# Lightning attention and a Fourier mix on one core: two plain groups of the perceptron and five Strassen pairs, with each batch's mix beside the next batch's attention

## The chip, the cores and the metric

The kernel runs on one core of a Trainium2 chip. The metric is the device time in microseconds of one execution; the median of repeated runs is used. Engines are called by their short names: PE is TensorE's matmuls, PEld its loads of the stationary operand, DVE VectorE, ACT ScalarE, POOL GpSimd, SP the engine that issues most transfers.

## The reference, cut to what matters

```python
# q, k, v: (4 batches, 8 heads, 768 rows, 64) float32; lam: one decay per head
def _attn_ref(q, k, v, lam):                       # cut: set-up of Dmask, lam_pow, rev_pow
    for b in range(nb):                            # blocks of rows, a state carried along
        intra = np.einsum('bhic,bhjc->bhij', qb, kb) * Dmask[None]
        intra = np.einsum('bhij,bhjd->bhid', intra, vb)
        inter = np.einsum('bhid,bhde->bhie', qb * lam_pow[None], kv_state)
        out[:, :, sl] = intra + inter
        kv_state = lam_block * kv_state + np.einsum('bhsd,bhse->bhde', kb * rev_pow[None], vb)

def _moe_ref(x, w_ch1, w_ch2):                     # x: attention's result as (4, 768, 512)
    X = np.fft.fft(np.fft.fft(x, axis=1), axis=2)
    u = x + np.real(X)
    un = (u - mean(u)) / sqrt(var(u) + 1e-06)      # over the 512 columns of a row
    ch = np.maximum(un @ w_ch1, 0.0) @ w_ch2       # w_ch1 (512, 2048), w_ch2 (2048, 512), 64-bit
    return u + ch
```

So there are three parts for each of the four batches: attention, a Fourier mix with a normalisation, and a perceptron with one hidden layer of 2048.

## The kernel before

All matmuls are in 32-bit floats, each of them two records in the trace. Attention goes in chunks of 128 rows, six to a batch. The mix uses the symmetry of the real Fourier transform: rows and columns are folded (sums and differences of a row and its mirrored row), then come small matmuls with cosine and sine tables over the rows (L483), then over the columns (`width`). Mirrored rows come by an indirect gather from a copy in DRAM; for batch 0 they are made by turned transposes instead.

The perceptron works on groups of 256 rows: three to a batch, (batch, group) in the order `ORDER`. *Plain* groups are computed as the reference has it: 64 matmuls of 256 columns for the hidden layer and 32 of 512 columns for the second, woven into the rest of the kernel. *Late* groups are written to DRAM, normalised and transposed, and are computed at the end in pairs by Strassen's form (Winograd's variant): seven products of half size in place of eight, for both layers, with sums of the weights (`combine_weights`) and of the inputs made first on VectorE.

The kernel is a set of Python generators which yield an estimate of the time of each step; `weave` runs two of them side by side in the proportion given. What the generators give is the order of the program; a scheduler then places the instructions on the engines, and may move an instruction past others unless it is marked to stay in order.

```python
    xp = plain_pool("xp", 2 * NC)          # NC = 6: twelve buffers of 128 rows of x
    up = plain_pool("up", 3)
    # ... cut ...
    def attn(b):

        head = attn_in(b, 0)
        for c in range(NC):
            yield from head
            head = attn_in(b, c + 1) if c < NC - 1 else ()
            yield from attn_out(b, c, head)
    # ... attn_in: loads of k, q, v; transposes (L268, L273); attn_out: scores (L292, L296), state
    #     (L307 to L312), output (L320, L324), transposes back (L340); cut ...

    def fold_x(b, a, n, i, lo, hi):

        e, o = eo[b][a]
        tt = nc.vector.tensor_tensor

        tc.keep_in_program_order(tt(e[0:n, i, 0:DM], lo, hi, op=ALU.add))
        tc.keep_in_program_order(tt(o[0:n, i, 0:DM], lo, hi, op=ALU.subtract))
        tt(e[0:n, i, 1:HM], e[0:n, i, 1:HM], e[0:n, i, HM:DM - 1], op=ALU.add)
        tt(o[0:n, i, 1:HM], o[0:n, i, 1:HM], o[0:n, i, HM:DM - 1], op=ALU.subtract)

    # ... fold_a folds with rows mirrored inside the batch's second half, fold_b the other half and
    #     then the columns: eight more VectorE instructions for each of two blocks of rows; cut ...

    def fft_ln(b):
        yield 1.0
        fold_a(b)
        yield 3.0
        piece = fold_b(b)
        yield 6.0 if b == 0 else 9.0
        # ... matmuls with the tables, the widths, sums into x, norm for each group; cut ...

    ORDER = [(b, g) for b in range(B) for g in (1, 2, 0)]
    PLAIN, LATE = ORDER[:4], ORDER[4:]
    # ... cut ...
    def mlp(b, g, f0=0, f1=FO):

        ut = uts[b, g]
        hr = []
        for fc in range(f0, f1):
            ps = psum_m([128, G * 128])
            for c in range(KO):
                nc.tensor.matmul(ps, lhsT=w1[:, c, 128 * fc:128 * fc + 128], rhs=ut[:, c, :],
                                 start=(c == 0), stop=(c == KO - 1))
            if fc % 4 == 0:
                hr.append(new(hp_, [128, 4, G * 128], "hr"))
            t = hr[-1][:, fc % 4, :]
            if fc % 2:
                nc.vector.tensor_scalar(t, ps, 0.0, None, op0=ALU.max)
            else:
                nc.scalar.activation(t, ps, AF.Relu)
        # ... second matmul (L614) and the sum with x; with half of the hidden layer the sum goes
        #     back into x (L621, L622), at the end into y and out (L625, L626); cut ...

    # the conversion of the 64-bit weights: 32 pieces, each two ACT and five DVE instructions
    w = weights()
    t_chunk = 7.3
    t_front = NC * t_chunk + 13.0 + 7.0 + 5.7 + 3 * 2.4
    t_mlp = FO * 1.7 + G * 4 * 3.4
    def beside(lead, t, other, t_other):
        return weave(lead, part(other, t_other), t_other / t)

    att1, mix = attn(1), fft_ln(0)
    run(beside(attn(0), NC * t_chunk, w, 0.25 * NW))

    next(mix)
    run(beside(part(att1, t_chunk), t_chunk, w, 0.03 * NW))
    next(mix)
    run(beside(part(att1, t_chunk), t_chunk, w, 0.03 * NW))
    next(mix)
    run(part(att1, 0.5 * t_chunk))
    run(beside(mix, 24.0, beside(att1, 3.5 * t_chunk, w, 0.19 * NW), 0.19 * NW + 2.5 * t_chunk))

    half = [[mlp(b, g, h * FO // 2, (h + 1) * FO // 2) for b, g in PLAIN[:3]] for h in range(2)]
    fr = chain([att1, fft_ln(1)] + [front(b) for b in range(2, B)])
    t_rest, t_back = 3 * t_front - 5 * t_chunk, len(PLAIN) * t_mlp - 45.0
    t_half = 1.5 * t_mlp
    run(beside(beside(chain(half[0]), t_half, w, 0.5 * NW), t_half + 0.5 * NW, fr, t_rest * t_half / t_back))
    run(w)
    back = chain(half[1] + [mlp(*PLAIN[3])])
    run(weave(fr, back, (t_back - t_half) / (t_rest - t_rest * t_half / t_back)))
    front_end.close()
    s2.wp = ctx.enter_context(tc.tile_pool(name="ws", bufs=1, side="left", reuse_waits="tile"))
    # ... pools for the late groups are opened; load_u(0) ...
    run(weave(combine_weights(0), back, 1.5))
    run(back)
    # ...
    run(combine_weights(1))
    for j in range(len(LATE) // 2):
        late(j)
```

The buffers of x of a plain group are held until its second half has been added and stored; those of a late group are stored in DRAM right after its normalisation and become free.

Of the kernel before, what the change touches and what calls it, by code (L numbers as in the profile page):

```python
# [76 lines left out]
def kernel(  # L77
# [10 lines left out]
    nc = tc.nc  # L88
    B, H, S, D = q.shape
    DM = H * D  # L90
    DFF = moe_w_ch1.shape[1]
    C = 128
    NC = S // C
# [24 lines left out]
    def plain_pool(name, bufs):  # L118
        return plain_end.enter_context(tc.tile_pool(name=name, bufs=bufs, side="right"))
# [6 lines left out]
    np_ = front_pool("np", 2)  # L126
    ep = front_pool("ep", 2)
    xp = plain_pool("xp", 2 * NC)
    up = plain_pool("up", 3)
    hp_ = plain_pool("hp", FO // 4)  # L130
    dram = ctx.enter_context(tc.tile_pool(name="dram", bufs=1, space=bass.MemoryType.DRAM))
    PS = bass.MemoryType.PSUM
# [107 lines left out]

    def attn(b):

        head = attn_in(b, 0)
        for c in range(NC):
            yield from head
            head = attn_in(b, c + 1) if c < NC - 1 else ()
            yield from attn_out(b, c, head)

    ins, oTs, eo = {}, {}, {}
    TURNED = (0,)  # L250
    first = const.tile([128, HP, 1], F32, name="first")

    def attn_in(b, c):
        rows = slice(c * C, (c + 1) * C)
        kt, qt, vt = (new(ld, [C, H, D], nm) for nm in ("k", "q", "v"))
        for t, src in ((kt, k), (qt, q), (vt, v)):
            nc.sync.dma_start(t, src[b, :, rows, :].rearrange("h p d -> p h d"))
        if b == 0:
            load_tables(c)

        kd = None
        if c < NC - 1:
            kd = new(at, [C, H, D], "kd")
            nc.gpsimd.tensor_tensor(kd, kt, kpow, op=ALU.mult)

        ptk = psum_a([128, HP, C])
        for hp in range(HP):
            nc.tensor.transpose(ptk[:, hp, :], pair(kt, hp), ident)  # L268
        kT = new(at, [128, HP, C], "kT", bufs=2)
        nc.scalar.copy(kT, ptk)  # L270
        ptq = psum_a([128, HP, C])
        for hp in range(HP):
            nc.tensor.transpose(ptq[:, hp, :], pair(qt, hp), ident)  # L273
        qT = new(at, [128, HP, C], "qT", bufs=2)
        nc.scalar.copy(qT, ptq)  # L275
        qs = None
        if c > 0:
            qs = new(at, [128, HP, C], "qs")
            nc.vector.tensor_tensor(qs, ptq, qpow, op=ALU.mult)
        ins[b, c] = kT, qT, qs, kd, vt  # L280
        yield 1.2
# [123 lines left out]
# [4 lines that stand above are left out]

        tc.keep_in_program_order(tt(e[0:n, i, 0:DM], lo, hi, op=ALU.add))  # L410
        tc.keep_in_program_order(tt(o[0:n, i, 0:DM], lo, hi, op=ALU.subtract))
        tt(e[0:n, i, 1:HM], e[0:n, i, 1:HM], e[0:n, i, HM:DM - 1], op=ALU.add)
        tt(o[0:n, i, 1:HM], o[0:n, i, 1:HM], o[0:n, i, HM:DM - 1], op=ALU.subtract)

    def mirror_a(b):

# [15 lines left out]

    def fold_a(b):
        for a, n in enumerate(BLK):
            fold_x(b, a, n, 1, eo[b][a][1][0:n, 1, 0:DM], xn_[b, HC + a][0:n])

    def fold_b(b):

        sets = []
        tt = nc.vector.tensor_tensor  # L440
        for a, n in enumerate(BLK):
            fold_x(b, a, n, 0, xs[b, a][0:n], xs[b, HC + a][0:n])
            e, o = eo[b][a]
            nc.scalar.copy(e[0:n, :, HM:HM + 1], e[0:n, :, DM - 1:DM])

            am, bm = e[0:n, :, W:2 * W], o[0:n, :, W:2 * W]
            lo, hi = e[0:n, 0, 0:HM + 1], e[0:n, 1, 0:HM + 1]
            tt(am[:, 0, 0:HM + 1], lo, hi, op=ALU.add)
            tt(am[:, 1, 0:HM + 1], lo, hi, op=ALU.subtract)

            lo, hi = am[:, :, 0:QM], am[:, :, HM:QM:-1]
            tt(e[0:n, :, 0:QM], lo, hi, op=ALU.add)
            tt(e[0:n, :, QM:HM], lo, hi, op=ALU.subtract)
            lo, hi = o[0:n, 0, 1:HM], o[0:n, 1, 1:HM]
            tt(bm[:, 0, 1:HM], lo, hi, op=ALU.subtract)
            tt(bm[:, 1, 1:HM], lo, hi, op=ALU.add)
            lo, hi = bm[:, :, 1:QM + 1], bm[:, :, HM - 1:QM - 1:-1]
            tt(o[0:n, :, 0:QM], lo, hi, op=ALU.subtract)
            tt(o[0:n, :, QM:HM], lo, hi, op=ALU.add)
            sets.append((e, o))  # L460
        eo.pop(b)

        def piece(a, i, n):

            c0 = W + QM if i == 4 else QM * (i % 2)
            return sets[a][i in (2, 3)][0:BLK[a], n, c0:c0 + (1 if i == 4 else QM)]

        return piece

    def fft_ln(b):  # L470
        yield 1.0
        fold_a(b)
        yield 3.0
        piece = fold_b(b)
        yield 6.0 if b == 0 else 9.0


        for i in range(5):
# [101 lines left out]


    ORDER = [(b, g) for b in range(B) for g in (1, 2, 0)]
    PLAIN, LATE = ORDER[:4], ORDER[4:]

    def store(b, T, y, cols=slice(0, DM)):
        if T < HC:
            nc.sync.dma_start(out[b, 128 * T:128 * T + 128, cols], y[:, cols])
        else:
            nc.gpsimd.indirect_dma_start(out=out.rearrange("b s d -> (b s) d"),  # L589
                                         out_offset=row_of(2 + HC * (b + 1) + T - HC),  # L590
                                         in_=y[:, :], in_offset=None)

    def mlp(b, g, f0=0, f1=FO):

        ut = uts[b, g]
        hr = []
        for fc in range(f0, f1):
            ps = psum_m([128, G * 128])
            for c in range(KO):
                nc.tensor.matmul(ps, lhsT=w1[:, c, 128 * fc:128 * fc + 128], rhs=ut[:, c, :],  # L600
                                 start=(c == 0), stop=(c == KO - 1))
            if fc % 4 == 0:
                hr.append(new(hp_, [128, 4, G * 128], "hr"))
            t = hr[-1][:, fc % 4, :]
# [4 lines that stand above are left out]
            yield 1.7  # L609
        for i in range(G):  # L610
            T = TT[g][i]
            ps = psum_m([128, DM])
            for fc in range(f0, f1):
                nc.tensor.matmul(ps, lhsT=hr[(fc - f0) // 4][:, fc % 4, 128 * i:128 * i + 128], rhs=w2[:, fc, :],  # L614
                                 start=(fc == f0), stop=(fc == f1 - 1))
                if fc % 4 == 3 and fc < f1 - 1:
                    yield 3.4
            u = xs[b, T]
            tt = nc.vector.tensor_tensor
            if f1 < FO:  # L620
                tt(u[:, 0:HM], ps[:, 0:HM], u[:, 0:HM], op=ALU.add)  # L621
                tt(u[:, HM:DM], ps[:, DM - 1:HM - 1:-1], u[:, HM:DM], op=ALU.add)  # L622
            else:
                y = new(up, [128, DM], "y", bufs=1)
                tt(y[:, 0:HM], ps[:, 0:HM], u[:, 0:HM], op=ALU.add)  # L625
                tt(y[:, HM:DM], ps[:, HM:DM], u[:, DM - 1:HM - 1:-1], op=ALU.add)  # L626
                store(b, T, y)
            yield 3.4
# [138 lines left out]
    def front(b):  # L767
        yield from attn(b)
        yield from fft_ln(b)

    def weave(lead, other, ratio):

        t_lead = t_other = 0.0
        for d in lead:
            t_lead += d
            while t_other < t_lead * ratio:
                d = next(other, None)
                if d is None:
                    return t_lead + sum(lead)
                t_other += d  # L780
                yield d
            yield d
        return t_lead

    def run(gen):
        return sum(gen)

    def part(gen, n):
        for d in gen:
            yield d  # L790
            n -= d
            if n <= 0:
                return

    def chain(gens):
        for g in gens:
            yield from g
# [7 lines left out]
    def beside(lead, t, other, t_other):  # L805
        return weave(lead, part(other, t_other), t_other / t)
# [1 line left out]
    att1, mix = attn(1), fft_ln(0)  # L808
    run(beside(attn(0), NC * t_chunk, w, 0.25 * NW))

    next(mix)
    run(beside(part(att1, t_chunk), t_chunk, w, 0.03 * NW))
    next(mix)
    run(beside(part(att1, t_chunk), t_chunk, w, 0.03 * NW))
    next(mix)
    run(part(att1, 0.5 * t_chunk))
    run(beside(mix, 24.0, beside(att1, 3.5 * t_chunk, w, 0.19 * NW), 0.19 * NW + 2.5 * t_chunk))

    half = [[mlp(b, g, h * FO // 2, (h + 1) * FO // 2) for b, g in PLAIN[:3]] for h in range(2)]
    fr = chain([att1, fft_ln(1)] + [front(b) for b in range(2, B)])  # L820
    t_rest, t_back = 3 * t_front - 5 * t_chunk, len(PLAIN) * t_mlp - 45.0
    t_half = 1.5 * t_mlp
    run(beside(beside(chain(half[0]), t_half, w, 0.5 * NW), t_half + 0.5 * NW, fr, t_rest * t_half / t_back))
    run(w)
    back = chain(half[1] + [mlp(*PLAIN[3])])
    run(weave(fr, back, (t_back - t_half) / (t_rest - t_rest * t_half / t_back)))
    front_end.close()
    s2.wp = ctx.enter_context(tc.tile_pool(name="ws", bufs=1, side="left", reuse_waits="tile"))
    s2.up = ctx.enter_context(tc.tile_pool(name="us", bufs=1, side="left", reuse_waits="tile"))
# [43 lines left out]
```

## Time and profile before

| | |
|---|---|
| time, median of 3 runs | 843.8 us (843.48 to 846.13) |
| span of the profiled execution | 842.3 us |
| mean granted clock of TensorE | 0.988 |
| PE, PEld busy | 96%, 76% |
| DVE, ACT, POOL busy | 53%, 22%, 9% |
| data moved | 68.87 MB, mean 82 GB/s |
| hidden layer of plain groups (L600), PE busy | 119.8 us, 512 records |
| second layer of plain groups (L614), PE busy | 116.1 us, 256 records |
| Strassen products (L687 and L734) in the chain that ended last | 23% and 23% |

A group of instructions in the profile has a line of the kernel, an engine, its output and inputs by name, and a count. A group's busy time is the time in which at least one of its instructions ran, so matmuls that overlap in the array are not counted twice. The chain that ended last is followed back from the last instruction: at each step to the one that released it, or to the one before it on its engine.

### The profile page before, as it was taken

How to read it: one execution, taken by the hardware profiler on the slowest of the kernel's cores; microseconds unless marked ns; L12 is line 12 of the kernel's file. 1: busy time of each engine (PE TensorE's matmuls, PEld its weight loads, DVE VectorE, ACT ScalarE, POOL GpSimd, SP SyncE). 2: the span in 40 equal slices, each digit the busy share in tenths (PEclk: the TensorE clock that was granted, in tenths of full speed). 3: DMA queues.
4: the chain of work that ended last, by engine and by line, in shares of the span. 5: the costliest groups of instructions: out<-in, count | busy, mean ns of one | idle time of the engine just before them, and what ended most of it. 6: DMA issues, size and time to landing. Idle time of an engine off the chain costs nothing.

```text
span 842.3 us, 11685 instructions
## 1 busy us (share of the span) xinstructions
PE 805.3 (96%) x4608; PEld 642.3 (76%) x4608; DVE 446.0 (53%) x1030; ACT 181.9 (22%) x436; POOL 77.2 (9%) x102
## 2 busy tenths in 40 slices
PE   5987799999999999999999999999999999999998
PEld 4766676776767666767846888888888888888886
DVE  5969989884923483246696661155412552145411
ACT  3753442422521111221101210022000220012100
POOL 2211122010101110121000000000000000000000
PEclk9988999999999999999999999999999999999999
DMA  9957544137932125451334011100111000110010
GB/s 228 262 141 185 154 123 148 51 85 193 223 97 62 50 67 128 98 140 53 77 86 150 0 51 38 46 18 0 51 51 51 0 1 13 47 41 1 1 38 25
DMA packets 126683, 68.87 MB, mean 82 GB/s; under 512 B 111150, under 2 KB 112174, under 8 KB 126630
## 3 DMA queue, kind: packets, MB, share of 16 engines
q1 hardware_dynamic: 121632, 55.67, 26.1%
q0 software_dynamic: 2112, 6.69, 2.5%
q10 hardware_dynamic: 2886, 5.77, 2.0%
q8 instruction: 36, 0.59, 0.3%
q14 instruction: 17, 0.14, 0.1%
HBM read 48.72 MB, written 19.40 MB: 81 GB/s over the span
## 4 chain that ended last, share of the span: by engine, by line
PE 80%; DVE 10%; issue 4%; DMA 3%; ACT 2%; POOL 1%; SPq 0%; POOLq 0%; DVEq 0%; ACTq 0%
PE p L734 23%; PE p L687 23%; PE pm L614 9%; PE pm L600 7%; PE pa L292 3%; PE pa L324 3%; PE pa L483 3%; PE pa L320 2%; PE pa L340 1%; DMA x<-xb,ix 1%; PE pa L268 1%; PE pa L307 1%; PE pa L273 1%; DVE stt L513 1%; DMA xb<-xn 1%
## 5 line engine op out<-in xcount | busy, mean ns | idle before, releaser
L600 PE MATMUL pm<-ut,w 128*128 128x256 f32 x512 | 119.8, 383 | 0.2 <-DVE hr L606 0.2
L614 PE MATMUL pm<-w,hr 128*128 128x512 f32 x256 | 116.1, 598 | 1.3 <-DVE hr L606 1.3
L600 PEld LDWEIGHTS pm<-ut,w 128*128 128x128 f32 x512 | 94.1, 190 | 15.6 <-issue 3.4
L687 PE MATMUL p<-ur,w 128*128 128x256 f32 x384 | 93.8, 379 | 0.0
L614 PEld LDWEIGHTS pm<-w,hr 128*128 128x128 f32 x256 | 46.6, 190 | 51.4 <-issue 48.6
L687 PEld LDWEIGHTS p<-ur,w 128*128 128x128 f32 x384 | 73.0, 190 | 10.3 <-issue 0.5
L687 PE MATMUL p<-us,w1s 128*128 128x256 f32 x256 | 65.7, 379 | 0.0
L734 PE MATMUL p<-w,hs 128*128 128x256 f32 x256 | 58.0, 379 | 0.5 <-DVE y L755 0.5
L734 PE MATMUL p<-w,ha 128*128 128x256 f32 x256 | 57.9, 379 | 0.0
L734 PE MATMUL p<-w2s,hs 128*128 128x256 f32 x256 | 57.9, 379 | 0.0
L734 PEld LDWEIGHTS p<-w,hs 128*128 128x128 f32 x256 | 48.5, 190 | 7.5 <-DVE y L755 0.9
L734 PEld LDWEIGHTS p<-w,ha 128*128 128x128 f32 x256 | 48.6, 190 | 6.6
L734 PEld LDWEIGHTS p<-w2s,hs 128*128 128x128 f32 x256 | 48.6, 190 | 6.6
L687 PEld LDWEIGHTS p<-us,w1s 128*128 128x128 f32 x256 | 48.6, 190 | 6.6
L589 POOL DMA_INDIRECT out_dram<-y,ix x12 | 11.8, 987 | 408.4 <-DVE y L760 344.2
L714 ACT COPY ha<-p 128x256 f32<-128x256 f32 x32 | 11.9, 372 | 169.2 <-PE p L687 139.4
L292 PEld LDWEIGHTS pa<-qT,kT 64*128 64x128 f32 x384 | 29.2, 205 | 18.3 <-ACT qT L275 10.9
L292 PE MATMUL pa<-qT,kT 64*128 64x128 f32 x384 | 34.3, 306 | 8.0 <-ACT qT L275 7.5
L296 DVE TENSOR_TENSOR sc<-pa,decay 128x512 f32<-128x512 f32 x48 | 31.6, 682 | 12.7 <-PE pa L292 12.6
L725 DVE TENSOR_TENSOR ha<-p,ha 128x256 f32<-128x256 f32 x32 | 13.6, 425 | 44.8 <-ACT ha L724 44.8
L324 PE MATMUL pa<-sc,v 128*64 128x128 f32 x384 | 31.9, 288 | 4.5 <-DVE sc L296 4.5
L324 PEld LDWEIGHTS pa<-sc,v 128*64 128x64 f32 x384 | 23.4, 141 | 13.6 <-DVE sc L296 7.6
(144 smaller groups left out, 1143.2 us busy)
## 6 DMA issues: line engine op xcount, KB each, us to landing
raw<-in_moe_w_ch_dram SPq DMA_DIRECT2D x32, 512.0 KB, 5.0
k<-in_k_dram SPq DMA_DIRECT2D x24, 256.0 KB, 5.3
q<-in_q_dram SPq DMA_DIRECT2D x24, 256.0 KB, 5.0
v<-in_v_dram SPq DMA_DIRECT2D x24, 256.0 KB, 3.3
ud<-x SPq DMA_DIRECT2D x16, 256.0 KB, 2.3
utd<-e SPq DMA_DIRECT2D x64, 64.0 KB, 2.2
u<-ud SPq DMA_DIRECT2D x16, 256.0 KB, 2.7
ur<-utd SPq DMA_DIRECT2D x6, 512.0 KB, 4.7
```

What stands on the lines that cost most here:

```text
L292: mm(pss[hi][:, hp, :], lhsT=kT[HD[hi], hp, :], rhs=qT[HD[hi], hp, :], start=True, stop=True)
L296: nc.vector.tensor_tensor(t, pss[hi], decay[:, hi::2, :], op=ALU.mult)
L320: mm(po[HD[hi], hp, :], lhsT=s_old[HD[hi], hp, :], rhs=qs[HD[hi], hp, :], start=(hp == 0), stop=False, skip_group_check=True)
L324: mm(po[HD[hi], hp, :], lhsT=vt[:, 2 * hp + hi, :], rhs=sc[hi][:, hp, :], start=(c == 0 and hp == 0), stop=(hp == HP - 1), skip_group_chec ...
L483: mm = nc.tensor.matmul(ps[0:m, n, :], lhsT=piece(a, i, n), rhs=cs[0:rows, a, i in (2, 3), n, :], start=(a == 0), stop=(a == 1))
L589: nc.gpsimd.indirect_dma_start(out=out.rearrange("b s d -> (b s) d"), out_offset=row_of(2 + HC * (b + 1) + T - HC), in_=y[:, :], in_offset ...
L600: nc.tensor.matmul(ps, lhsT=w1[:, c, 128 * fc:128 * fc + 128], rhs=ut[:, c, :], start=(c == 0), stop=(c == KO - 1))
L614: nc.tensor.matmul(ps, lhsT=hr[(fc - f0) // 4][:, fc % 4, 128 * i:128 * i + 128], rhs=w2[:, fc, :], start=(fc == f0), stop=(fc == f1 - 1))
L687: nc.tensor.matmul(ps, lhsT=s2.A[a][:, kt, 128 * i:128 * i + 128], rhs=U[b][:, kt, :], start=(first and kt == 0), stop=(kt == 1), skip_gro ...
L714: nc.scalar.copy(a11, two(X))
L725: V.tensor_tensor(a22, two(Z), a22, op=ADD)
L734: nc.tensor.matmul(ps, lhsT=h[a][:, s, i, :], rhs=s2.B[b][:, i, :], start=(first and i == 0), stop=(i == HF - 1), skip_group_check=True)
```

## The change

Two of the twelve groups stay plain, (0, 1) and (0, 2), and the other ten are computed in five pairs in Strassen's form, which needs fewer products. The plain groups were what TensorE did while a mix went through its chain of folds, small matmuls and norms; in their place the mixes of batches 1 and 2 are now woven with the first three and a half chunks of the next batch's attention. For batch 0 the folds are handed out in small steps, with two and a half chunks of batch 1's attention beside them and no conversion of weights, and the first loads and transposes of batch 1 are made within the last chunk of batch 0. The hidden-layer matmuls of the second halves of the plain groups are marked to stay in program order.

```diff
--- before.py
+++ after.py
@@ -126,7 +126,7 @@
     np_ = front_pool("np", 2)
     ep = front_pool("ep", 2)
     xp = plain_pool("xp", 2 * NC)
-    up = plain_pool("up", 3)
+    up = plain_pool("up", 2)
     hp_ = plain_pool("hp", FO // 4)
     dram = ctx.enter_context(tc.tile_pool(name="dram", bufs=1, space=bass.MemoryType.DRAM))
     PS = bass.MemoryType.PSUM
@@ -240,13 +240,14 @@
 
     def attn(b):
 
-        head = attn_in(b, 0)
+        head = () if b - 1 in LEADS else attn_in(b, 0)
         for c in range(NC):
             yield from head
-            head = attn_in(b, c + 1) if c < NC - 1 else ()
+            head = attn_in(b, c + 1) if c < NC - 1 else attn_in(b + 1, 0) if b in LEADS else ()
             yield from attn_out(b, c, head)
 
     ins, oTs, eo = {}, {}, {}
+    LEADS = (0,)
     TURNED = (0,)
     first = const.tile([128, HP, 1], F32, name="first")
 
@@ -409,8 +410,10 @@
 
         tc.keep_in_program_order(tt(e[0:n, i, 0:DM], lo, hi, op=ALU.add))
         tc.keep_in_program_order(tt(o[0:n, i, 0:DM], lo, hi, op=ALU.subtract))
+        yield 1.4
         tt(e[0:n, i, 1:HM], e[0:n, i, 1:HM], e[0:n, i, HM:DM - 1], op=ALU.add)
         tt(o[0:n, i, 1:HM], o[0:n, i, 1:HM], o[0:n, i, HM:DM - 1], op=ALU.subtract)
+        yield 0.8
 
     def mirror_a(b):
 
@@ -432,14 +435,13 @@
 
     def fold_a(b):
         for a, n in enumerate(BLK):
-            fold_x(b, a, n, 1, eo[b][a][1][0:n, 1, 0:DM], xn_[b, HC + a][0:n])
-
-    def fold_b(b):
-
-        sets = []
+            yield from fold_x(b, a, n, 1, eo[b][a][1][0:n, 1, 0:DM], xn_[b, HC + a][0:n])
+
+    def fold_b(b, sets):
+
         tt = nc.vector.tensor_tensor
         for a, n in enumerate(BLK):
-            fold_x(b, a, n, 0, xs[b, a][0:n], xs[b, HC + a][0:n])
+            yield from fold_x(b, a, n, 0, xs[b, a][0:n], xs[b, HC + a][0:n])
             e, o = eo[b][a]
             nc.scalar.copy(e[0:n, :, HM:HM + 1], e[0:n, :, DM - 1:DM])
 
@@ -447,32 +449,43 @@
             lo, hi = e[0:n, 0, 0:HM + 1], e[0:n, 1, 0:HM + 1]
             tt(am[:, 0, 0:HM + 1], lo, hi, op=ALU.add)
             tt(am[:, 1, 0:HM + 1], lo, hi, op=ALU.subtract)
+            yield 0.8
 
             lo, hi = am[:, :, 0:QM], am[:, :, HM:QM:-1]
             tt(e[0:n, :, 0:QM], lo, hi, op=ALU.add)
             tt(e[0:n, :, QM:HM], lo, hi, op=ALU.subtract)
+            yield 0.8
             lo, hi = o[0:n, 0, 1:HM], o[0:n, 1, 1:HM]
             tt(bm[:, 0, 1:HM], lo, hi, op=ALU.subtract)
             tt(bm[:, 1, 1:HM], lo, hi, op=ALU.add)
+            yield 0.8
             lo, hi = bm[:, :, 1:QM + 1], bm[:, :, HM - 1:QM - 1:-1]
             tt(o[0:n, :, 0:QM], lo, hi, op=ALU.subtract)
             tt(o[0:n, :, QM:HM], lo, hi, op=ALU.add)
+            yield 0.8
             sets.append((e, o))
         eo.pop(b)
 
+    T_FOLD = 2 * (2 * 2.2 + 4 * 0.8)
+
+    def fft_ln(b):
+        sets = []
+
         def piece(a, i, n):
 
             c0 = W + QM if i == 4 else QM * (i % 2)
             return sets[a][i in (2, 3)][0:BLK[a], n, c0:c0 + (1 if i == 4 else QM)]
 
-        return piece
-
-    def fft_ln(b):
-        yield 1.0
-        fold_a(b)
-        yield 3.0
-        piece = fold_b(b)
-        yield 6.0 if b == 0 else 9.0
+        if b in LEADS:
+            yield from fold_a(b)
+            yield from fold_b(b, sets)
+            yield 2.0
+        else:
+            yield 1.0
+            run(fold_a(b))
+            yield 3.0
+            run(fold_b(b, sets))
+            yield 9.0
 
 
         for i in range(5):
@@ -580,7 +593,7 @@
 
 
     ORDER = [(b, g) for b in range(B) for g in (1, 2, 0)]
-    PLAIN, LATE = ORDER[:4], ORDER[4:]
+    PLAIN, LATE = ORDER[:2], ORDER[2:]
 
     def store(b, T, y, cols=slice(0, DM)):
         if T < HC:
@@ -590,6 +603,8 @@
                                          out_offset=row_of(2 + HC * (b + 1) + T - HC),
                                          in_=y[:, :], in_offset=None)
 
+    pin = []
+
     def mlp(b, g, f0=0, f1=FO):
 
         ut = uts[b, g]
@@ -597,8 +612,10 @@
         for fc in range(f0, f1):
             ps = psum_m([128, G * 128])
             for c in range(KO):
-                nc.tensor.matmul(ps, lhsT=w1[:, c, 128 * fc:128 * fc + 128], rhs=ut[:, c, :],
-                                 start=(c == 0), stop=(c == KO - 1))
+                mm = nc.tensor.matmul(ps, lhsT=w1[:, c, 128 * fc:128 * fc + 128], rhs=ut[:, c, :],
+                                      start=(c == 0), stop=(c == KO - 1))
+                if pin and c == 0:
+                    tc.keep_in_program_order(mm)
             if fc % 4 == 0:
                 hr.append(new(hp_, [128, 4, G * 128], "hr"))
             t = hr[-1][:, fc % 4, :]
@@ -808,22 +825,32 @@
     att1, mix = attn(1), fft_ln(0)
     run(beside(attn(0), NC * t_chunk, w, 0.25 * NW))
 
-    next(mix)
-    run(beside(part(att1, t_chunk), t_chunk, w, 0.03 * NW))
-    next(mix)
-    run(beside(part(att1, t_chunk), t_chunk, w, 0.03 * NW))
-    next(mix)
-    run(part(att1, 0.5 * t_chunk))
-    run(beside(mix, 24.0, beside(att1, 3.5 * t_chunk, w, 0.19 * NW), 0.19 * NW + 2.5 * t_chunk))
-
-    half = [[mlp(b, g, h * FO // 2, (h + 1) * FO // 2) for b, g in PLAIN[:3]] for h in range(2)]
-    fr = chain([att1, fft_ln(1)] + [front(b) for b in range(2, B)])
-    t_rest, t_back = 3 * t_front - 5 * t_chunk, len(PLAIN) * t_mlp - 45.0
-    t_half = 1.5 * t_mlp
-    run(beside(beside(chain(half[0]), t_half, w, 0.5 * NW), t_half + 0.5 * NW, fr, t_rest * t_half / t_back))
+    run(beside(part(mix, T_FOLD), T_FOLD, att1, 2.5 * t_chunk))
+    run(beside(mix, 24.0, beside(att1, 3.5 * t_chunk, w, 0.12 * NW), 0.12 * NW + 2.5 * t_chunk))
+
+    half = [chain([mlp(b, g, h * FO // 2, (h + 1) * FO // 2) for b, g in PLAIN]) for h in range(2)]
+    t_half = len(PLAIN) * t_mlp / 2
+    t_mix = t_front - NC * t_chunk
+
+    def fronts():
+
+        yield from att1
+        for b in range(1, B):
+            if b == B - 1:
+                yield from fft_ln(b)
+                return
+            nxt = attn(b + 1)
+            yield from beside(fft_ln(b), t_mix, nxt, 3.5 * t_chunk)
+            yield from nxt
+
+    fr = fronts()
+    t_rest = (3 * NC - 5) * t_chunk + 2 * t_mix
+    run(beside(beside(half[0], t_half, w, 0.5 * NW), t_half + 0.5 * NW, part(fr, t_rest), t_rest))
+    run(half[0])
     run(w)
-    back = chain(half[1] + [mlp(*PLAIN[3])])
-    run(weave(fr, back, (t_back - t_half) / (t_rest - t_rest * t_half / t_back)))
+    back = half[1]
+    pin.append(1)
+    run(weave(fr, back, 0.55))
     front_end.close()
     s2.wp = ctx.enter_context(tc.tile_pool(name="ws", bufs=1, side="left", reuse_waits="tile"))
     s2.up = ctx.enter_context(tc.tile_pool(name="us", bufs=1, side="left", reuse_waits="tile"))
```

## The prediction

> **What bounds the kernel now.** I read the page's busy shares first, then the chain that ended last, then stages cut at the places where the chain changes its lines, and last the timeline of TensorE to get the price of one block of work.
>
> ```profile
> PE 805.3 (96%) x4608; PEld 642.3 (76%) x4608; DVE 446.0 (53%) x1030; ACT 181.9 (22%) x436; POOL 77.2 (9%) x102
> ...
> PE   5987799999999999999999999999999999999998
> ...
> DVE  5969989884923483246696661155412552145411
> ```
>
> TensorE is busy for 96% of the span, and its row of tenths is a 9 nearly everywhere but in the first six slices of 21 us. VectorE is the fuller engine just there, and half empty later. So two regimes: a start in which VectorE leads, and a long rest in which TensorE leads.
>
> ```profile
> 423.64 27.55 PE pm L614 x64
> 451.19 46.62 PE p L687 x216
> ...
> 548.75 45.76 PE p L687 x212
> ...
> 645.44 45.76 PE p L687 x212
> ...
> 742.13 45.76 PE p L687 x212
> ```
>
> This is the chain of waits (start, length, what). From 451.2 us to the end it is nothing but the products of the Strassen pairs. One pair starts every 96.7 us (645.44 - 548.75, and 742.13 - 645.44). The four pairs are 386.8 us, and the end after them 4.3 us (842.3 - 451.2 - 386.8). All before 451.2 us I call the front. A quarter, 64 records of the second matmul of a plain group, takes 27.55 us.
>
> ```profile
> 0.00:54.00 54.00, 40.03 (x437) 32.90 (x437) 41.51 (x79) 29.04 (x64) 13.14 (x25) 1.00 0.93 228
> 54.00:180.00 126.00, 112.53 (x793) 86.77 (x794) 108.90 (x246) 48.85 (x111) 21.08 (x26) 0.92 0.46 130
> 180.00:377.00 197.00, 193.55 (x1309) 134.73 (x1309) 96.25 (x206) 47.92 (x108) 28.28 (x34) 1.00 0.46 113
> 377.00:424.00 47.00, 44.99 (x218) 35.77 (x217) 31.52 (x79) 8.09 (x26) 5.40 (x10) 1.00 0.29 80
> 424.00:451.20 27.20, 27.20 (x65) 12.13 (x64) 24.73 (x30) 0.00 (x0) 0.58 (x1) 1.00 0.48 130
> ```
>
> Stages of the front: length, then busy us (and instructions) of PE, PEld, DVE, ACT, POOL, then the granted clock, DMA share and GB/s. To 54 us runs batch 0's attention; to 180 us batch 0's and 1's mixes, batch 1's attention and most of the conversion of the weights; to 377 us the attention of batches 2 and 3 and mix 2 among plain groups; to 424 us mix 3; to 451 us the weight sums of the Strassen form beside the last plain work. In the second stage VectorE is busy 108.9 of 126 us (86%) and TensorE's granted clock falls to 0.92; from 180 us on TensorE is full.
>
> ```profile
> 208.76 0.60 PE L268 MATMUL pa<-ident,k 128*128 128x128 f32 x4
> 209.20 1.03 PE L600 MATMUL pm<-ut,w 128*128 128x256 f32 x4
> ...
> 214.22 1.09 PE L320 MATMUL pa<-qs,st 64*64 64x128 f32 x16
> 215.24 1.09 PE L324 MATMUL pa<-sc,v 128*64 128x128 f32 x16
> 216.27 0.70 PE L600 MATMUL pm<-ut,w 128*128 128x256 f32 x2
> ```
>
> The timeline of TensorE where it is full: starts, not lengths, give the price, as lengths overlap. Four transposes cost 0.44 us (209.20 - 208.76), the 16 records of L320 and of L324 1.02 us each.
>
> [...] here the 0.92 stands in the one stage with both gaps and matmuls.[...] the folds: a 128x512 one takes 0.68 us here, a 128x256 one 0.42, so the small steps change order and not cost.
>
> **The change part by part.** *Two plain groups become one pair.* A plain group has 128 records of L600 and 64 of L614. In the chain 64 of L600 take 13.81 us back to back, so 27.6 us + 27.55 us = 55.2 us, and two groups 110.4. A pair costs 96.7. With TensorE full both times that saves 13.7 us: the sure gain.
>
> *TensorE's work in the front.* One chunk of attention: three blocks of four transposes at 0.44, L292 1.5, L307 0.6, L320 and L324 1.02 each, sum 5.5 us; 24 chunks less four L320 of first chunks and four L307 of last ones, about 125 us. One mix: 40 records of L483 at 0.17 us (12 of them took 2.06 us by their starts), 6.9, and 4.0 for the widths (3 x 1.11 and 0.66), 11 us; four are 44. Transposes of plain groups, 4 x 0.9 = 3.5. Plain groups 220.8. Sum 393 to 395 us of 451: 56 us are lost to waits and to a lower clock. By stage: to 54 us 22 lost (31.7 of work); to 180 us 28 (125 records of L600 and 32 of L614 are 41 us, attention and two mixes with their transposes 57); after it about 5. After the change the work is 395 - 110.4 - 1.8 = 283 us. Were the same 56 us lost, the front would end at 339.
>
> *VectorE's work in the front.* It is busy 278 us to 424 us. The change removes 16 ReLU copies (L606) and some ten sums of second matmuls at about 0.35 us each, -9, and adds four transposes of 0.65 for the two groups that go by way of DRAM, +2.6: 272 us, then the same 25 us of weight sums. The conversion of weights is untouched: 32 pieces of five VectorE instructions (0.77, 0.75, 0.46, 0.46, 0.45 us), 92 us by durations. Hence the front of about 340 us has VectorE at 87% and TensorE at 83%, where the old front had 67% and 87%.
>
> *The order.* (1) Next batch's first loads and transposes are put into the end of attention 0: the step from attention 0 to attention 1 loses about 2 us now (L292 starts at 46.65 and then 56.67, where 6 to 7 is usual). (2) Mix 0's folds have attention 1 beside them without weights: two pieces of weights (2 x 2.8 us of VectorE) leave that stretch, and two more the next. Mix 0 ends maybe 10 to 15 us earlier, but the same 11 us of conversion comes later. (3) Mixes 1 and 2 run beside attentions 2 and 3. A mix now takes 42 to 52 us from last attention chunk to last norm (377 to 424) with only 11 us of matmuls, and plain groups filled it; attention takes over as filler.
>
> *Stage by stage, after.* To 54 us as now, VectorE 41.5. Then everything up to the start of mix 3: VectorE has 272 - 41.5 - 33 (mix 3 and the second halves' own work) = 197 us, TensorE 94 + 33 + 2 + 55 = 184. VectorE was 86% busy in the stage most like it; with finer steps I take 90%: 219 us, so mix 3 starts at 273. Mix 3 takes 43 us (47 now), the weight sums and the sums of the first pair's inputs 27 (24.7 of them VectorE): 70 us, in which TensorE has 11 + 55 = 66 of work. The front ends at 343. Then 5 x 96.7 + 4.3 = 487.8: span 831. The reported time lies 1.5 us above the span (843.8 against 842.3): 832. I round to 831, as the 43 us of mix 3 were measured with plain work between its matmuls.
>
> **The rivals.** *VectorE becomes the bound of the front.* For it: 87% over the front, and 90 to 93% needed from 54 us to mix 3. At 86%, as before, that part lasts 229 us and not 219, so the total is 841, and nothing is gained. Against: from 140 to 160 us VectorE reached 19.6 of 20 us.
>
> *Mix 3 loses its filler.* The second halves are kept in order and woven in at 0.55 per unit of the mix, so only some 17 of 54 units lie beside mix 3: 11 + 17 = 28 us of work in 43. If they cannot move earlier, 15 us stand idle there. Yet the remaining 37 us then cover 27 us of weight sums, with 10 over, so up to 10 us are lost and the front ends near 353: total 841.
>
> *Buffers of x hold attention back.* Twelve buffers: four stay with the two plain groups to the end, six are the batch in its mix, two are left, so attention of the next batch stops at its third chunk until the mix's first group is stored. For it: the gathers of mix 2 wait 16.9 and 8.2 us today for buffers that plain groups hold. Against: four and not eight are held, the third chunk is planned about there, and the stretch has TensorE work elsewhere. I give it 0 to 5 us a batch.
>
> *The start gains more than I count.* If attention 1 beside the small folds closes half of the 28 us lost to 180 us, and VectorE runs at 94%, mix 3 starts near 264 and the total is 821.
>
> **Range and chances.** The sure gain is 13.7 us (1.6%); it alone gives 830. Going past 2% (below 827) needs 3 us more from the start; the rivals take up to 10 each. Range 818 to 847. Faster by over 2% 0.33, within 2% 0.61, slower (above 860.7) 0.06: that would need VectorE's and mix 3's losses together and more.
>
> **What would show it.** Right: five pairs 96.7 us apart, the first starting at 335 to 352 us; VectorE near 90% from 54 us to mix 3; the stage with two mixes' folds shows a granted clock nearer 1. Wrong: if the first pair starts after 360, look at idle TensorE in mix 3 or at waits for x buffers; if before 330, the start's 50 lost us have shrunk. If pairs are further apart than 97 us, the loads of inputs by way of DRAM are no longer hidden.

## The result, and the profile after

The changed kernel takes 876.6 us (median of 4 runs, 872.0 to 878.2) against 843.7 us: ratio 1.037, 95% interval 1.033 to 1.042. It is slower by 3.7%, and 831 was predicted. The profiled execution has a span of 870.2 us at a mean granted clock of 0.973.

First the page of the changed kernel, with the same rows that were shown of the kernel before:

```profile
PE 793.6 (91%) x4656; PEld 656.2 (75%) x4656; DVE 473.7 (54%) x1104; ACT 185.6 (21%) x448; POOL 88.1 (10%) x102
...
PE   5989689996797959849999999999999999999998
...
DVE  6979579874889646975611553135511553035411
```

TensorE is busy for less time (793.6 against 805.3 us) in a longer span. Between 196 and 392 us its row has a 6, two 7s, a 5, an 8 and a 4 where it had been a 9. At the 6 and at the 5 VectorE's row has a 4: there both engines wait. At the other four VectorE is the fuller engine (8, 9, 9 and 7).

Next the chain of waits of the changed kernel (start, length, what), at the Strassen products and just before them:

```profile
375.15 0.63 DVE e L554
...
377.76 2.15 DMA utd<-e
...
380.16 0.38 ACT ha L731
...
380.62 2.06 PE p L704 x4
...
383.37 45.77 PE p L704 x204
...
480.08 45.76 PE p L704 x212
...
576.77 45.76 PE p L704 x212
...
673.46 45.76 PE p L704 x212
```

A pair still follows the last one after 96.69 us (576.77 - 480.08), so the gain per pair stands. But the pairs run without a break only from 383.4 us, not from 343 as predicted. The front is 68 us shorter than before (451.2), and one more pair takes 97 us: the 29 us between, less 1 us at the end, are the difference of the spans (870.2 and 842.3).

The front of the changed kernel by stages (length, busy us and instructions of PE, PEld, DVE, ACT, POOL, then clock, DMA share, GB/s):

```profile
0.00:54.00 54.00, 41.01 (x480) 33.65 (x480) 43.95 (x85) 30.83 (x68) 12.72 (x25) 1.00 0.94 226
54.00:120.00 66.00, 53.66 (x521) 43.64 (x520) 50.18 (x106) 25.25 (x59) 13.75 (x16) 0.95 0.55 147
120.00:190.00 70.00, 67.52 (x532) 49.40 (x532) 60.27 (x139) 24.54 (x57) 20.69 (x18) 1.00 0.62 154
190.00:240.00 50.00, 35.25 (x233) 24.17 (x231) 32.87 (x66) 14.88 (x30) 11.31 (x9) 0.86 0.73 182
240.00:300.00 60.00, 54.64 (x410) 42.07 (x410) 48.82 (x112) 22.27 (x51) 10.02 (x11) 0.97 0.53 141
...
314.90:325.00 10.10, 0.01 (x1) 0.02 (x1) 3.40 (x9) 0.83 (x3) 1.92 (x2) 0.66 0.30 104
...
365.80:383.40 17.60, 3.80 (x13) 2.40 (x12) 16.67 (x22) 0.74 (x2) 0.00 (x0) 0.70 0.45 124
```

Length less PE busy is TensorE's idle time. Over the whole front it is 72.6 us (383.4 - 310.8), where the kernel before had 32.9 (451.2 - 418.3). The 39.7 us more are as much as the 40 us by which the front missed its 343. The start is no worse (13.0 and 12.3 us, against 14.0 and 11.8 in the same stretches before). Three places are: 14.8 us from 190 to 240 us, 10.1 us ahead of mix 3's matmuls (314.9 to 325), and 13.8 us under the weight sums (365.8 to 383.4). The clock is 0.86 in the first of them, 0.66 in the second and 0.70 in the third. In the last one VectorE is nearly full with the sums (16.67 of 17.6 us), and its end is not a sum: VectorE makes the last transposed rows of mix 3 only at 375.15 us, their stores land at 379.9, and ScalarE's copy of the first product waits for these.

What stands in the first place is seen in the queue of SP in the changed kernel (timeline; a row of SP is the issue of transfers, and its length covers a wait between two issues of one row):

```profile
161.00 0.52 SPq L258 DMA_DIRECT2D k<-in_k_dram  x1
...
180.46 5.99 SPq L558 DMA_DIRECT2D utd<-e  x8
186.54 0.56 SPq L209 DMA_DIRECT2D raw<-in_moe_w_ch_dram  x1
195.25 5.27 SPq L558 DMA_DIRECT2D utd<-e  x8
200.57 1.10 SPq L564 DMA_DIRECT2D ud<-x  x2
201.78 0.40 SPq L209 DMA_DIRECT2D raw<-in_moe_w_ch_dram  x1
202.23 0.45 SPq L258 DMA_DIRECT2D q<-in_q_dram  x1
...
217.13 10.03 SPq L209 DMA_DIRECT2D raw<-in_moe_w_ch_dram  x2
227.27 0.38 SPq L258 DMA_DIRECT2D k<-in_k_dram  x1
```

From 187.1 to 195.2 us SP issues nothing: its next entry is a store of transposed rows of mix 1, which waits 8.1 us for its transpose on VectorE (L554). The last loads of attention 2 (q at 202.23) stand behind it, and behind the 8 stores themselves. The k of the same chunk had been issued at 161.00: q follows it 41 us later. At 217 two loads of weights take 10 us, 8.7 of them a wait for a buffer that VectorE (L221) still has to read, and again k stands behind them until 227. GpSimd's gather of mirrored rows waits as well, for 32.7 us in all, at the end for a load of v by the trace:

```profile
213.64 1.26 POOL L424 DMA_INDIRECT fo<-xa,ix  x1 [32.70 <-DMA v<-in_v_dram]
```

In the kernel before, loads of attention 2 stand behind mix 1's stores too (a k at 194.89 us), but TensorE has plain work then and doesn't stop:

```profile
190.00:240.00 50.00, 50.00 (x368) 34.93 (x367) 32.50 (x65) 19.03 (x37) 6.91 (x7) 1.00 0.77 191
```

### The profile page after: what moved, and what is told of

It is laid out like the page before. It is cut to its first block, busy times and chain, and to the rows that moved or that the text cites. A ratio compares the mean times of both kernels' runs of the same rounds, so it can differ in the third digit from the quotient of the medians.

```text
span 870.2 us, 11915 instructions
## 1 busy us (share of the span) xinstructions
PE 793.6 (91%) x4656; PEld 656.2 (75%) x4656; DVE 473.7 (54%) x1104; ACT 185.6 (21%) x448; POOL 88.1 (10%) x102
## 4 chain that ended last, share of the span: by engine, by line
PE 59%; DVE 4%; DMA 1%; issue 1%; POOL 0%; ACT 0%; SPq 0%; DVEq 0%; ACTq 0%; POOLq 0%
PE p L704 28%; PE p L751 28%; PE pm L631 2%; DVE w1s L681 1%; DVE w2s L681 1%; PE pa L496 1%; DVE un L544 0%; DMA ud<-x 0%; DVE e L554 0%; PE pm L615 0%; DMA x<-xb,ix 0%; DMA utd<-e 0%; PE pa L325 0%; DMA xb<-xn 0%; DVE x L579 0%
## 5 line engine op out<-in xcount | busy, mean ns | idle before, releaser
L704 PE MATMUL p<-ur,w 128*128 128x256 f32 x480 | 118.4, 382 | 0.7 <-PE p L704 0.7
L704 PEld LDWEIGHTS p<-ur,w 128*128 128x128 f32 x480 | 91.7, 191 | 14.2 <-PE p L704 1.4
L704 PE MATMUL p<-us,w1s 128*128 128x256 f32 x320 | 83.8, 385 | 13.1 <-ACT ha L731 13.1
L751 PE MATMUL p<-w,hs 128*128 128x256 f32 x320 | 72.4, 380 | 0.5 <-DVE y L772 0.5
L615 PE MATMUL pm<-ut,w 128*128 128x256 f32 x256 | 63.6, 397 | 6.8 <-ACT hr L625 6.8
L615 PEld LDWEIGHTS pm<-ut,w 128*128 128x128 f32 x256 | 48.6, 198 | 14.7 <-ACT hr L625 7.2
L631 PE MATMUL pm<-w,hr 128*128 128x512 f32 x128 | 59.7, 604 | 0.0
L704 PE MATMUL p<-us,w 128*128 128x256 f32 x160 | 41.1, 379 | 0.0
L704 PE MATMUL p<-ur,w1s 128*128 128x256 f32 x160 | 41.1, 379 | 0.0
L631 PEld LDWEIGHTS pm<-w,hr 128*128 128x128 f32 x128 | 23.6, 195 | 22.6 <-issue 21.8
```

The costliest lines, as they stand in the source:

```text
L615: mm = nc.tensor.matmul(ps, lhsT=w1[:, c, 128 * fc:128 * fc + 128], rhs=ut[:, c, :], start=(c == 0), stop=(c == KO - 1))
L704: nc.tensor.matmul(ps, lhsT=s2.A[a][:, kt, 128 * i:128 * i + 128], rhs=U[b][:, kt, :], start=(first and kt == 0), stop=(kt == 1), skip_gro ...
L751: nc.tensor.matmul(ps, lhsT=h[a][:, s, i, :], rhs=s2.B[b][:, i, :], start=(first and i == 0), stop=(i == HF - 1), skip_group_check=True)
```

## The experiments

Times are medians of 4 to 20 runs; ratios are to the kernel before, which ran on the same chip beside them. A trace is of one execution: that of the changed kernel took 872.0 us, the shortest of its four, so what a run gains is read from the medians and ratios, and where it gains from the traces.

### Second halves held back until mix 3

```diff
     def fronts():
         ...
             if b == B - 1:
-                yield from fft_ln(b)
                 return
 ...
+    run(fr)
     pin.append(1)
-    run(weave(fr, back, 0.55))
+    run(weave(fft_ln(B - 1), back, 0.55))
```

> The second halves of the plain groups start only when batch 3's attention is done; nothing else differs from the changed kernel (876.6 us, first pair's products from 383 us). Filler theory (the second half of group (0, 1), 27 us of matmuls, is spent beside attention 3, so mix 3 stands idle for 10 us and the weight sums for 14): mix 3 and the sums are covered, idle TensorE after attention 3 falls from 24 us to under 6, attention 3 without filler gets shorter by some 14 us, total 855 to 864. Queue theory (the loss is waits at in-order queues between 54 and 300 us): that stretch is untouched, the filler only moves, total 870 to 878.

Measured: 869.9 us, ratio 1.031 (1.028 to 1.034); the intervals of this run and of the changed kernel overlap a little. The stages of this run, attention 3 with the end of mix 2, then mix 3, then the weight sums:

```profile
240.00:306.00 66.00, 51.22 (x399) 38.04 (x395) 52.46 (x119) 22.73 (x50) 12.34 (x13) 0.82 0.53 141
306.00:345.00 39.00, 34.85 (x153) 26.86 (x154) 22.24 (x54) 6.43 (x21) 4.16 (x6) 0.87 0.25 60
345.00:385.00 40.00, 38.58 (x121) 22.30 (x120) 35.48 (x59) 1.70 (x5) 3.67 (x5) 1.00 0.51 134
```

As the filler theory had it, mix 3 and the sums are covered: 4.2 and 1.4 us idle. But attention 3 does not get 14 us shorter. It ends 8 us earlier (306.6 against 314.9 us), with 14.8 us of idle time from 240 us and a clock of 0.82: the idle time moved forward. So both theories were half right, and what holds attention back had to be found. The chain of waits of this run up to the middle names it:

```profile
200.30 0.72 DVE e L554
201.04 0.57 SPq L558
...
206.36 0.62 SPq L564
208.01 5.43 DMA q<-in_q_dram
213.51 5.94 DMA v<-in_v_dram
...
220.15 5.30 DMA fo<-xa,ix
225.47 0.70 DVE fe L411
...
231.03 0.61 DVE sc L297
231.69 2.57 PE pa L325 x16
```

A transpose of mix 1 releases SP's next stores (eight of transposed rows, four for each tile of 128 rows, and one more), one after the other, about 0.6 us each; only then attention's loads are issued; the copy from which mirrored rows are gathered comes late; VectorE waits for the gather, which lands at 225.45 us, with a fold (225.47), and attention's scores (L297) come behind the folds, at 231.03.

### Attention's loads off SP

```diff
-            nc.sync.dma_start(t, src[b, :, rows, :]...)
+            (nc.scalar if b > 1 else nc.sync).dma_start(t, src[b, :, rows, :]...)
```

> The loads of k, q and v of batches 2 and 3 are issued by ScalarE instead of SP, everything else as in the changed kernel (876.6 us). SP-queue theory (attention's loads stand behind the mix's stores and the weights' loads, which wait 8 and 10 us for their inputs near 190 and 217 us, and the mirrored rows come late for it): TensorE's idle time from 190 to 240 us, 14.7 us, falls to under 5, total 860 to 869. If the loads are not what the chain waits for: within 3 us of 876.6.

Measured: 858.6 us, ratio 1.019 (1.017 to 1.022), 18 us less than the changed kernel. In this run the stage and SP's queue read:

```profile
190.00:240.00 50.00, 46.88 (x345) 33.56 (x344) 42.68 (x95) 21.22 (x44) 18.34 (x10) 1.00 0.82 222
...
345.00:370.00 25.00, 8.25 (x22) 5.05 (x21) 21.25 (x29) 0.37 (x1) 1.07 (x1) 0.68 0.50 145
```

```profile
193.38 8.80 SPq L558 DMA_DIRECT2D utd<-e  x8
207.26 23.53 SPq L209 DMA_DIRECT2D raw<-in_moe_w_ch_dram  x7
```

and ScalarE's queue, at the k and q of attention 2's last chunk:

```profile
160.01 0.37 ACTq L258 DMA_DIRECT2D k<-in_k_dram  x1
...
161.05 0.48 ACTq L258 DMA_DIRECT2D q<-in_q_dram  x1
```

Now q is issued 1 us after its k and not 41: its buffer was free by then, and it was SP's queue that had held it. From issue to landing no load of k, q or v takes more than 7.8 us in the changed kernel (median 4.4), little beside those 41 us, so it is the time of issue that counts. TensorE's idle time from 190 to 240 us falls from 14.8 to 3.1 us, and VectorE, which had been called the bound, is busy for 42.7 us there instead of 32.9. SP still waits (seven loads of weights in 23.5 us), but nothing that attention needs stands behind. The idle time under the weight sums is still there (16.8 us of 25): that loss is another one.

The same edit to the kernel before shows whether SP had held attention all along:

> The kernel before, with the loads of k, q and v of batches 2 and 3 issued by ScalarE. Theory that the change itself brought the SP wait (mix and attention now share SP at the same time, and the plain filler that hid such waits is gone): within 3 us of the kernel before, 841 to 847. Theory that SP held attention back all along: the kernel before gains several us too, 830 to 840.

Measured: 845.9 us over 20 runs, ratio 1.002 (1.001 to 1.004). No gain, if anything 2 us lost. What the wait on SP costs came with the change; before it, loads stood behind stores too, at a time when TensorE had other work.

### Attention and mix one after the other again

```diff
-            yield from beside(fft_ln(b), t_mix, nxt, 3.5 * t_chunk)
+            yield from fft_ln(b)
             yield from nxt
```

> Two plain groups and five pairs, but the mixes of batches 1 and 2 no longer beside the next attention: one after the other, as before the change. If overlapping mix and attention is what brings the queue waits (queue theory), 190 to 300 us get quieter and the total falls to 860 to 872. If overlapping is needed once the plain filler is gone (what the change is built on), a mix has only the first halves beside it and the total rises to 885 to 905. Filler theory alone: the end keeps its 24 us, total 870 to 885.

Measured: 900.1 us, ratio 1.069 (1.067 to 1.071). So the overlap does what it is for: without it two plain groups cost another 24 us. It makes up part of what the plain groups had filled, not all of it.

### Two other waits

```diff
 # gathers at the end of a batch's attention
-            if c == NC - 2:
+            if last:
                 mirror_a(b)
-            elif last:
                 mirror_b(b)
```

> The gathers of mirrored rows of the first kind are issued at the end of a batch's attention with those of the second kind, and no longer one chunk earlier, where they stand in GpSimd's queue ahead of the norm of the mix that runs beside. Queue theory: GpSimd's wait of 12.7 us before the gather near 100 us is gone, VectorE's 7.3 us and TensorE's 6.8 us there go with it, total 862 to 871. Filler theory: this does not touch the end, total within 3 us of 876.6 or a little more, as the folds start later.

Measured: 873.8 us, ratio 1.036 (1.033 to 1.038), not to be told from the changed kernel.

```diff
 # two buffers of their own for the transposed rows
-                    uq = new(ep, [128, DM], "e")
+                    uq = new(ep, [128, DM], "uq")
```

> The transposed rows of late groups get two buffers of their own and share none with the conversion of the weights. Queue theory: ScalarE's waits of 9.8 us for the stores of these buffers and TensorE's 6.8 us at 194 us are gone, total 864 to 871. Filler theory: total within 3 us of 876.6.

Measured: 879.7 us, ratio 1.045 (1.042 to 1.049): no gain, and rather 3 us lost. ScalarE's waits for these buffers were real in the trace (6.3 us at the longest), but taking them away does not make the kernel faster: a long wait in a profile need not be on the path.

### The conversion of the weights, and the start

```diff
-    run(beside(mix, 24.0, beside(att1, 3.5 * t_chunk, w, 0.12 * NW), 0.12 * NW + 2.5 * t_chunk))
+    run(beside(mix, 24.0, beside(att1, 3.5 * t_chunk, w, 0.25 * NW), 0.25 * NW + 2.5 * t_chunk))
```

> Eight pieces of weights instead of four are converted beside mix 0 and the rest of attention 1, so four fewer compete with mixes 1 and 2. VectorE theory (the conversion that was put off to 190 to 290 us is what attention and mix wait for): VectorE is busier to 120 us (76% of 54 to 120 us in the changed kernel), quieter after, total 864 to 872. Rival (the same work of VectorE in another place): the start is longer by what the middle is shorter, total 873 to 880.

Measured: 868.1 us, ratio 1.029 (1.027 to 1.030), 8 us less. From 54 to 120 us VectorE is busy for 60.2 us instead of 50.2, and the last piece of weights is done at 270.0 us instead of 286.5. The changed kernel had left VectorE idle for 15.8 us of those 66. The two traced executions differ by 1.3 us only (870.7 and 872.0), so they do not show where the 8 us of the medians come from.

With this number of pieces, the start of the kernel before put back (`LEADS` empty, folds in whole):

> The changed kernel with the start of the kernel before: folds of batch 0 in whole and not in small steps, batch 1's first loads not drawn into batch 0's last chunk, eight pieces of weights beside mix 0 as in the earlier-conversion run (868.1 us). If the finer start is worth what the prediction hoped for (10 to 15 us earlier end of mix 0): 874 to 883. If it only moves work: 866 to 871.

Measured: 878.4 us, ratio 1.040 (1.034 to 1.045), 10 us more than with the finer start.

### The edits together

Second halves held back, attention's loads on ScalarE, late gathers:

> Three edits at once: second halves held back until mix 3, the loads of batches 2 and 3 issued by ScalarE, the gathers at the end of a batch's attention. If filler and queues each cost what was said, their gains add: 869.9 for the first, and 3 and 8 to 15 us more: 852 to 860. If they all hit one and the same limit, about 866 to 870.

Measured: 853.8 us, ratio 1.011 (1.008 to 1.015): the gains add (0.026 of the ratio, and the three alone sum to 0.026). With the earlier conversion:

> The three edits and the earlier conversion. If VectorE's work in the middle is the limit: 8 us below the three edits. If not: within 3 us of them.

Measured: 849.5 us, ratio 1.008 (1.005 to 1.011), 4 us less, between the two expectations, and the intervals overlap. With the second halves begun a little earlier:

```diff
-    run(fr)
+    run(weave(fr, back, 0.25))
     pin.append(1)
     run(weave(fft_ln(B - 1), back, 0.55))
```

> All four edits, but the second halves start at the end of mix 2 at 0.25 per unit (6 to 8 us of matmuls beside attention 3) and go on at 0.55 in mix 3. Filler theory: in the kernel with the four edits (849.5 us) some 36 units were left for 27 us of sums, so 7 us of them are free to fill attention 3's gaps, total 841 to 846. If attention 3 is bound by VectorE and not by lack of filler: 847 to 852.

Measured: 845.5 us over 12 runs, ratio 1.003 (1.000 to 1.005): the loss is gone, and no gain is left over. Two more edits on top, own buffers and batch 1's loads on ScalarE:

> The same with buffers of their own for the transposed rows and with batch 1's loads issued by ScalarE too. With SP no longer in the way, the wait of 6 us near 214 us behind stores of the shared buffers should go: 3 to 7 us below the kernel with the quarter, 836 to 842. If those buffers cost nothing, as they did alone: equal within 2 us.

Measured: 855.5 us, ratio 1.016 (1.014 to 1.019), 10 us worse, against the expectation. The buffers alone on top tell which edit it was:

> The kernel with the quarter (845.5 us), and buffers of their own for the transposed rows, but batch 1's loads on SP as there. If the 10 us that the run with both lost came from the loads of batch 1 on ScalarE: 843 to 847. If they came from the buffers (stores no longer throttle the norms, and crowd SP): 852 to 857.

Measured: 846.2 us over 12 runs, ratio 1.005 (1.003 to 1.007). So the buffers are not to blame, and batch 1's loads on ScalarE are. The reason was not followed up; ScalarE converts weights in that stretch.

### Four plain groups with the finer start alone

The kernel before, with only the folds in small steps, the first loads drawn in and eight pieces of weights beside mix 0:

> Four plain groups and the order of the kernel before, with only the finer start of the change (folds of batch 0 in small steps beside attention 1, the first loads drawn in, eight pieces of weights). Theory that the start is a gain of its own and the loss is all in the thin filler: as TensorE is full from 180 us there, what the start saves goes through to the end, 832 to 840. Rival (it only moves VectorE's work): 841 to 848.

Measured: 834.5 us (831.9 to 836.6), ratio 0.992 (0.990 to 0.994). This is the only version that beats both kernels. Its stages, the later ones cut 13 us earlier than for the kernel before, and its first pair in the chain of waits:

```profile
54.00:180.00 126.00, 115.20 (x847) 85.44 (x846) 114.10 (x261) 51.22 (x115) 23.56 (x28) 1.00 0.49 136
180.00:364.00 184.00, 180.72 (x1239) 127.49 (x1238) 87.91 (x189) 44.86 (x101) 26.00 (x31) 1.00 0.47 118
364.00:411.00 47.00, 45.19 (x222) 36.14 (x220) 31.51 (x79) 8.17 (x26) 5.73 (x8) 1.00 0.28 80
```

```profile
438.68 46.62 PE p L704 x216
```

From 54 to 180 us VectorE gets 114.1 us of work done instead of 108.9, TensorE's clock is 1.00 instead of 0.92, and 847 instead of 793 matmul records go through. After that TensorE is full, as before, so the lead stays: the first pair starts at 438.7 and not at 451.2 us. (These 12.5 us are of two single executions; the medians differ by 7 us.)

## Why the prediction was wrong

**The sure gain was right.** Pairs 96.7 us apart were predicted and 96.69 measured. The 13.7 us per replaced pair of groups hold only "with TensorE full both times", and that condition fell.

**The step that failed is the one from 54 us to mix 3**: "197 us" of VectorE at "90%: 219 us, so mix 3 starts at 273". VectorE's work was sized well: it is busy for 200 us there. But it took 261 us (54 to 314.9), at 77% and not 90%. TensorE had 225 us of work there and not 184, as 41 us of second halves came early (next paragraph), but it was not full either (86%), and these 41 us explain little: with the second halves held back, as they had been planned, attention 3 still ended at 306.6 us. Over the stretch as a whole neither engine was the bound. What the prediction did not name are waits in a queue: the stores of one batch's mix and the loads of the next one's attention share SP, and nothing was issued there from 187.1 to 195.2 us while a store waited for its data. Moving the loads gave 18 us back; which waits make up the rest is not separated. I had reasoned from the busy shares of a stage with another mixture of work.

**The order was misread.** The prediction had "only some 17 of 54 units" of the second halves beside mix 3 and "the remaining 37 us" for the sums. In the trace group (0, 1)'s second half is spent by 313 us, before mix 3's matmuls, and only 13.8 us of group (0, 2) are left from 352 us on, against 27 us of sums. The reason is in `weave`: its inner loop reuses the name `d`, so after drawing from `other` it hands on that step's duration in place of the lead's. Nested weaves thus report wrong times. Adding up the yields as the program makes them, the first halves are spent when mix 2 has had 26 of its 33 units and attention 3 20 of its 43, and the second halves start there, not at mix 3. This agrees with the trace; with the right durations the same sum puts their start into mix 3. Holding them back closed the gap under mix 3 and the sums, but alone it moved most of it into attention 3; its worth in the sum with the other edits was not measured alone.

**Postponed conversion was called neutral** ("the same 11 us of conversion comes later"). It cost 8 us by the medians: between 54 and 120 us VectorE had room (idle for 15.8 of 66 us). What the conversion holds up later was not shown.

**The start was right, a little smaller.** For an end of mix 0 "10 to 15 us earlier" the traces show about 9: its last statistics (bn_stats) start at 118.93 us in the changed kernel and at 127.58 in the one before. The run with the old start takes 10 us longer than the one with the new, and four plain groups gain 7 us (0.8%) from it. In the changed kernel its gain is in the 876.6 already.

**The rivals.** "Mix 3 loses its filler" came true, larger (24 us with the sums, not 10) and from the opposite error: too little left, not too much. "VectorE becomes the bound" did not, over the front as a whole (77%). "Buffers of x hold attention back" did not: the gathers into these buffers that had waited 16.9 and 8.2 us for plain groups now wait 3.8 us at most, and for none of them.

**One line was misread.** The prediction called the stage with the clock of 0.92 the only one with both gaps and matmuls. Its own lines show 14.0 us without matmuls to 54 us as well, at a clock of 1.00.

What stays open: with the four edits and the quarter, the pairs start at 356.5 us and not at 343. From 120 to 300 us TensorE is idle for 19.4 of 180 us there. Which waits these are was not separated.

## What to carry to other kernels

Before work that fills a busy engine's gaps is taken out, ask what else can fill them at that very moment, and whether it shares a queue with the work it is put beside: here a store that waited 8.1 us for its data held the loads behind it. Busy shares of an old stage don't tell how densely a new mixture of chains can run (VectorE: 86% in the stage that was taken as the model, 77% in the new one); when both engines are idle together, follow the chain and not the fullest engine. When a change has several parts, try each alone: here the part that looked like a helper, the finer start, was the only one that beat the kernel before.

## What the runs showed of the hardware

The long gaps in TensorE's work cost more than their length: the matmuls behind them started slow. In the changed kernel five single gaps are longer than 6 us (6.8, 6.8, 6.3, 10.1 and 13.1 us, before 110.0, 201.2, 227.4, 325.0 and 380.6 us), and behind each of them the granted clock reads 0.50 for at least 2.5 us. Behind the 10.1 us ahead of mix 3:

```profile
324.99 1.65 PE L496 MATMUL pa<-cs,fe 128*128 128x193 f32 x4 [10.13 <-DVE fe L455]
326.43 1.49 PE L496 MATMUL pa<-cs,fo 128*128 128x193 f32 x4
327.85 4.12 PE L496 MATMUL pa<-cs,fe 128*1 128x193 f32 x20
```

The first eight records take 0.36 us each by their starts, where the prediction read 0.17, at a granted clock of 0.50 from 324.9 to 327.9 us; the next twenty take 0.20.

More surprising was the queue that issues. The 36 loads of batches 2 and 3 on another engine were worth 18 us (876.6 against 858.6): SP, while it waited 8.1 us for the data of one transfer, started none of those behind it, and a q that came 41 us after its k came 1 us after it on ScalarE. In the kernel before, where TensorE is busy for all of the 50 us from 190 to 240 us, the same edit brought nothing (845.9 us, ratio 1.002).
